# Two adds of the attention's sum over keys become one step of the instruction planner

## The chip, the cores and the metric

The kernel runs on one core of a Trainium2 chip. Its time is the device time of one execution in microseconds (us); a kernel's time is the median of several runs. The core has five engines with an instruction queue each, which start their instructions in the order of the program: TensorE (PE in the profile, with PEld for its weight loads), VectorE (DVE), ScalarE (ACT), GpSimd (POOL) and SyncE (SP), which here issues the DMAs. An engine that reaches an instruction whose input is not there yet waits, and all that stands behind it in its queue waits too.

## What is computed

The input is 2048 tokens of 640 numbers in float32. Two layers follow each other, each an attention block and a channel MLP, both with a residual. All four blocks use the same kinds of steps, and both layers the same weights:

```python
def _A_ref(x, wqkv, wo):            # attention: 32 heads of 20, window of 8 keys, every second token
    W, dil = 8, 2
    qkv = transpose((x @ wqkv).reshape(B, S, 3, H, Dh))
    q, k, v = qkv[0], qkv[1], qkv[2]
    idx = pos[:, None] - (arange(W) * dil)[None, :]       # this token and the 7 at distances 2, 4, ... 14
    kg, vg = k[idx], v[idx]                               # masked where idx < 0
    attn = softmax(where(mask, einsum("bhsd,bhswd->bhsw", q, kg) * Dh ** -0.5, -1e9))
    o = einsum("bhsw,bhswd->bhsd", attn, vg)              # the sum over the 8 keys
    return o.reshape(B, S, D) @ wo

def _B_ref(x, w1, b1, w2, b2):      # MLP 640 -> 1536 -> 640
    h = gelu(layernorm(x) @ w1 + b1)
    return h @ w2 + b2

x = x + _A_ref(layernorm(x), A_wqkv, A_wo)
x = x + _B_ref(layernorm(x), B_w1, B_b1, B_w2, B_b2)
x = x + _A_ref(layernorm(x), A_wqkv, A_wo)
x = x + _B_ref(layernorm(x), B_w1, B_b1, B_w2, B_b2)
```

## The kernel before

**Tiling.** Since the window takes every second token, even and odd tokens never meet in the attention. The tokens are cut into four units of 512, two of even and two of odd tokens (`UNITS`); on each of the 128 partitions lie four tokens of a unit that follow each other. Two layers of four units give eight steps `n` of the attention, 0 to 7, and eight of the MLP, `b`. Each `n` is split into four groups of heads (160 columns each), which makes 32 attention steps `G = 4n + g`.

**Matrix products.** TensorE works in float16. Each float32 operand is split into a high and a low half and each product is taken as three (`PASS`): high by high, high by low, low by high. Per unit TensorE does the products for q, k and v (line 648 in `qkv`), the output projection (line 805 in `project`), and the MLP in twelve blocks of 128 hidden columns: line 871 multiplies into the block, line 892 out of it. The MLPs of the last two units are done together in a scheme with seven block products instead of eight (`pair`, lines 1073 and 1108), after everything else.

**The attention on VectorE.** q, k and v go from PSUM through ScalarE (line 665) to memory and come back with DMAs that put the keys of a window beside their query (`fetch`). Function `attention(G)` then works in two halves `a` of two tokens per partition. For each half it multiplies q by the keys (line 732, 2560 columns) and sums over the 20 columns of a head (line 736); for both halves together it does the softmax with short instructions (lines 741 to 751, the exponential on ScalarE at line 747); for each half it multiplies the weights with the values (line 758, 2560 columns) and then sums over the eight keys with three adds: 8 keys to 4 (1280 columns, line 766), 4 to 2 (640 columns, line 766), 2 to 1 (320 columns, line 770, which writes the result). Each add reads what the one before wrote. There are 64 such halves, so 64 adds of each size. The result is split into high (ScalarE, line 777) and low (line 780, on GpSimd for three groups in four, on VectorE for the fourth), transposed by DMAs (`project`, line 793), and goes into the projection.

**Other work on VectorE.** Between these steps stand the low halves of the MLP's hidden block (line 882, wanted by the third pass of line 892), the low halves of the layer norm's result (line 618, which a transposing DMA at line 620 takes to TensorE), of the weights (line 476), and some residuals (lines 814 and 936).

**What sets the order.** The order on every engine is laid out before the kernel is built, by the class `Plan`. The kernel hands it steps: an engine, a planned duration, a priority, what the step needs and gives, the buffers it uses, and a function that emits its instructions. `Plan.run` keeps a clock for each engine and picks step after step. A step that needs the result of another on the same engine may start 0.06 us after the other's planned end; for any step the key by which the choice is made is not below the engine's clock plus 0.05 us:

```python
w = w + (self.LAG["sp"] + self.SPARE[o["eng"]] if moved else self.LAG[e] if e != o["eng"] else 0.06 * (e != "pe"))
...
key = (max(t - o["wait"], clock[e] + 0.05), o["prio"], o["n"])
```

So directly behind a VectorE step whose result it needs, a step comes second to any other step that is ready, whatever the priorities. A step is one item of the plan however many instructions it emits; nothing is put between them. The planned duration of a VectorE instruction of n columns is `v_cost(n)`, that is 0.067 us plus n/960 us. Steps of the kinds in `PAIRS` (all adds of the sum are among them) are kept apart in the plan from the longer GpSimd steps; a GpSimd step of this kind is placed at the end of a run of such VectorE steps and is made to wait for the VectorE step before it. After the plan, all engines run in the planned order, each waiting for the real semaphores.

Of the names in the diff, `dve(n, prio, emit, need, give, use, more)` adds a VectorE step with duration `v_cost(n) + more`; `("pv", G, a)` is the product with the values, `("ad", G, a, w)` an add, `("o", G, a)` the finished half; `vk` is the buffer `pr` with the products (two of them), `ok` the result buffer, of the `w` buffers. `FILL` and `DRAIN` are priorities of two ScalarE steps of the MLP.

Of the kernel before, what the change touches and what calls it, by code (L numbers as in the profile page):

```python
# [20 lines left out]
GC = D // NG  # L21
# [15 lines left out]
EH = 2  # L37
# [28 lines left out]
PAIRS = ("qk", "pv", "ad", "o", "sub", "at", "hlo", "yl", "xb", "ol", "wq", "lo", "lm")  # L66

TURN = 2.7
FILL, DRAIN = -420, -700

THROUGH = (("sa", 29),)
LOP = ((29, -460),)
# [209 lines left out]
def v_cost(n):  # L282
    return 0.067 + n / 960.0
# [7 lines left out]
def sliding_dilated_then_mlp_kernel(  # L291
# [18 lines left out]
    nc = tc.nc  # L310
# [41 lines left out]
    def tile_of(pool, key):  # L352
        return T[pool][plan.slot[pool, key]]
# [63 lines left out]
    def dve(n, prio, emit, need=(), give=(), use=(), more=0.0, wait=None):  # L417
        plan.add("dve", v_cost(n) + more, prio, emit, need, give, use, wait=wait, pair=give[0][0] in PAIRS)
# [26 lines left out]
    def identity():  # L445
# [7 lines left out]
        give=["b1"])  # L453
    dma(320, 41, lambda: nc.sync.dma_start(b2, bass.AP(tensor=B_b2.tensor, offset=B_b2.offset, ap=[[0, P], [1, D]])),
        give=["b2"])
# [244 lines left out]
    def attention(G):  # L700
        n, g = divmod(G, NG)
        la, u = divmod(n, NU)
        par, start, m = UNITS[u]
        E = EH * W * GC
        L = m * W * GH
        NE = m // EH
        dve = partial(any_dve, wait=HURRY.get(G))
        wk, vw, ok, hk, sk = ("qk", G), ("v", G), ("w", ("o", G)), ("ohl", n), ("sm", G)

        def ot():  # L710
            return tile_of(*ok).rearrange("p (t c) -> p t c", t=m)

        def windows(w, t0, *dims):
            c = w[:, t0:t0 + EH]
            return bass.AP(tensor=c.tensor, offset=c.offset, ap=[list(c.ap[0]), [GC, EH], *dims])

        def lg(t0=0, t1=m):
            return tile_of(*sk)[:, t0 * W * GH:t1 * W * GH].rearrange("p (t w h) -> p t w h", t=t1 - t0, w=W)

        def lgt():  # L720
            return lg().rearrange("p t w h -> p t h w")

        def mx(j):
            return tile_of(*sk)[:, L + j * m * GH:L + (j + 1) * m * GH].rearrange("p (t h) -> p t h", t=m)

        for a in range(NE):
            t0 = a * EH
            pk = ("pr", (G, a, 0))

            def qk(t0=t0, pk=pk):  # L730
                w = tile_of(*wk)
                nc.vector.tensor_mul(tile_of(*pk), w[:, HALO + m + t0:HALO + m + t0 + EH, None, :].to_broadcast([P, EH, W, GC]),  # L732
                                     windows(w, t0, [GC, W], [1, GC]))

            dve(E, G - 0.6, qk, need=[("inq", G), ("ink", G)], give=[("qk", G, a)], use=[wk, pk, sk])
            dve(E, G - 0.7, lambda pk=pk, t0=t0: nc.vector.tensor_reduce(  # L736
                lg(t0, t0 + EH).rearrange("p t w h -> p (t w h)"), tile_of(*pk).rearrange("p t w (h d) -> p (t w h) d", d=DH),
                axis=AX.X, op=OP.add), need=[("qk", G, a)], give=[("lg", G, a)], use=[pk, sk])
        last = [("lg", G, a) for a in range(NE)]
        if start == 0:  # L740
            dve(L, G - 0.8, lambda: nc.vector.tensor_add(
                lg(), lg(), mask[:, :, :, None].to_broadcast([P, m, W, GH])), need=[*last, "mask"], give=[("lm", G)], use=[sk])
            last = [("lm", G)]
        dve(L, G - 0.8, lambda: nc.vector.tensor_reduce(mx(0), lgt(), axis=AX.X, op=OP.max), need=last, give=[("mx", G)], use=[sk], more=0.19)
        dve(L, G - 0.8, lambda: nc.vector.tensor_sub(lg(), lg(), mx(0)[:, :, None, :].to_broadcast([P, m, W, GH])),
            need=[("mx", G)], give=[("sub", G)], use=[sk])
        act(L, -450 + G, lambda: nc.scalar.activation(tile_of(*sk)[:, :L], tile_of(*sk)[:, :L], AF.Exp, scale=scale),
            need=[("sub", G)], give=[("e", G)], use=[sk], table="exp")
        dve(L, G - 0.8, lambda: nc.vector.tensor_reduce(mx(1), lgt(), axis=AX.X, op=OP.add), need=[("e", G)], give=[("s", G)], use=[sk], more=0.19)
        dve(8 * m * GH // 2, G - 0.8, lambda: nc.vector.reciprocal(mx(1), mx(1)), need=[("s", G)], give=[("rc", G)], use=[sk])  # L750
        dve(L, G - 0.8, lambda: nc.vector.tensor_mul(lg(), lg(), mx(1)[:, :, None, :].to_broadcast([P, m, W, GH])),
            need=[("rc", G)], give=[("at", G)], use=[sk])
        for a in range(NE):
            t0 = a * EH
            vk = ("pr", (G, a, 1))

            def pv(t0=t0, vk=vk):
                nc.vector.tensor_mul(  # L758
                    tile_of(*vk).rearrange("p t w (h d) -> p t (w h) d", d=DH),
                    lg(t0, t0 + EH).rearrange("p t w h -> p t (w h)")[:, :, :, None].to_broadcast([P, EH, W * GH, DH]),  # L760
                    windows(tile_of(*vw), t0, [DH, W * GH], [1, DH]))

            dve(E, G - 0.85, pv, need=[("at", G), ("inv", G)], give=[("pv", G, a)], use=[vw, sk, vk])
            last = ("pv", G, a)
            for w in (4, 2):
                dve(EH * w * GC, G - 0.9, lambda vk=vk, w=w: nc.vector.tensor_add(  # L766
                    tile_of(*vk)[:, :, 0:w], tile_of(*vk)[:, :, 0:w], tile_of(*vk)[:, :, w:2 * w]),
                    need=[last], give=[("ad", G, a, w)], use=[vk])
                last = ("ad", G, a, w)
            dve(EH * GC, G - 0.9, lambda vk=vk, t0=t0: nc.vector.tensor_add(  # L770
                ot()[:, t0:t0 + EH], tile_of(*vk)[:, :, 0], tile_of(*vk)[:, :, 1]),
                need=[last], give=[("o", G, a)], use=[vk, ok])

        def hi():
            return tile_of(*hk)[:, :, 0, g * GC:(g + 1) * GC]

        act(m * GC, -350 + G, lambda: nc.scalar.activation(hi(), ot(), AF.Copy),
            need=[("o", G, a) for a in range(NE)], give=[("oh", G)], use=[ok, hk])
        def lo(eng):
            eng.tensor_sub(tile_of(*hk)[:, :, 1, g * GC:(g + 1) * GC], ot(), hi())  # L780

        if g < NG - 1:
            pool(ASIDE, -300 + G, lambda: lo(nc.gpsimd), need=[("oh", G), ("qk", G + 1, 0)], give=[("ol", G)], use=[ok, hk],
                 pair=True)
        else:
            dve(m * GC, -300 + G, lambda: lo(nc.vector), need=[("oh", G)], give=[("ol", G)], use=[ok, hk])
# [43 lines left out]
    def mlp(at, b, t0, t1):  # L830
# [5 lines left out]
        last = ("acc4", at)  # L836
# [8 lines left out]
        def rest(i):  # L845
            return M, i * REST, BANK, REST

        filled = b > 2
        put = [("put2", b, i) for i in tiles] + [("put2", b, "rest")] if filled else []

        if filled:
            for i in tiles:
                act(BANK, FILL, lambda i=i: nc.scalar.activation(accs[i], x[u][:, i, :BANK], AF.Copy, scale=WS),
                    need=[("xb", b, i)] + [("out", b - 1, NF - 1, i)] * (b > 0), give=[("put2", b, i)], use=[bank(i)])
            act(REST * M, FILL, lambda: nc.scalar.activation(
                accs[M].rearrange("p (t c) -> p t c", c=REST), x[u][:, :, BANK:], AF.Copy, scale=WS),
                need=[("xb", b, i) for i in tiles] + [("out", b - 1, NF - 1, ("rest", at - 1))], give=[("put2", b, "rest")], use=[last])

        for e in range(NF):
# [3 lines left out]
            for i, k in enumerate((ck, wk)):  # L863
                dma(328, -250 + j + 1.5 * i, lambda k=k, i=i, e=e: nc.sync.dma_start(tile_of(*k), mw[i][e]),
                    need=[("mw", e, i)], give=[k], use=[k])

            def inner(ck=ck, pk=pk):
# [8 lines left out]
               use=[yk, ck, pk])  # L876
            act(nt, -430, lambda pk=pk, h32=h32, e=e: nc.scalar.activation(  # L877
                tile_of(*h32)[:, :nt], tile_of(*pk)[:, :nt], AF.Gelu_apprx_tanh, bias=b1[:, e:e + 1], scale=1.0 / WS),
                need=[("hp", j), "b1"], give=[("h", j)], use=[pk, h32], table="gelu", ptr=1)
            act(nt, -440, lambda h32=h32, hk=hk: nc.scalar.activation(tile_of(*hk)[:, 0, :nt], tile_of(*h32)[:, :nt], AF.Copy),  # L880
                need=[("h", j)], give=[("hhi", j)], use=[h32, hk])
            dve(nt, -1000, lambda h32=h32, hk=hk: nc.vector.tensor_sub(  # L882
                tile_of(*hk)[:, 1, :nt], tile_of(*h32)[:, :nt], tile_of(*hk)[:, 0, :nt]),
                need=[("hhi", j)], give=[("hlo", j)], use=[h32, hk])
# [11 lines left out]
            if e < NF - 1:  # L896
                for i in tiles:
                    prev = [("outh", b, e - 1, i)] if e else ([("outh", b, e, i - 1)] if i > t0 else [])
                    mm(2 * D, 4, j, lambda i=i, outer=outer: outer(i, PASS[:2], [own(i), rest(i)]), need=[("hhi", j), wk, *prev] + [("put2", b, i), ("put2", b, "rest")] * (filled and e == 0),
                       give=[("outh", b, e, i)], use=[wk, hk, bank(i), last])  # L900
                    mm(D, 2, j + 0.05, lambda i=i, outer=outer: outer(i, PASS[2:], [own(i), rest(i)]),
                       need=[("hlo", j), ("outh", b, e, i)], give=[("out", b, e, i)], use=[wk, hk, bank(i), last])
# [3 lines left out]
           need=[("hhi", j), wk, *before], give=[("outh", b, e, ("rest", at))], use=[wk, hk, last])  # L906
        mm(REST * len(tiles), len(tiles), j - 0.2, lambda: [outer(i, PASS[2:], [rest(i)]) for i in tiles],
           need=[("hlo", j), ("outh", b, e, ("rest", at))], give=[("out", b, e, ("rest", at))], use=[wk, hk, last])
        for i in tiles:
            mm(2 * BANK, 2, j, lambda i=i: outer(i, PASS[:2], [own(i)]),  # L910
               need=[("hhi", j), wk, *before], give=[("outh", b, e, i)], use=[wk, hk, bank(i)])
            mm(BANK, 1, j - 0.1, lambda i=i: outer(i, PASS[2:], [own(i)]),
               need=[("hlo", j), ("outh", b, e, i)], give=[("out", b, e, i)], use=[wk, hk, bank(i)])

        if filled:
            act(REST * M, DRAIN, lambda: nc.scalar.activation(
                x[u][:, :, BANK:], accs[M].rearrange("p (t c) -> p t c", c=REST), AF.Copy, scale=1.0 / WS),
                need=[("out", b, NF - 1, ("rest", at))], give=[("xr", la + 1, u, i) for i in tiles], use=[last])
        else:
            dve(REST * (t1 - t0), -991, lambda: add(  # L920
                x[u][:, t0:t1, BANK:], accs[M][:, t0 * REST:t1 * REST].rearrange("p (t c) -> p t c", c=REST)),
                need=[("out", b, NF - 1, ("rest", at)), *[("xb", b, i) for i in tiles]], give=[("xr", la + 1, u, i) for i in tiles],
                use=[last])
        for i in tiles:
            if filled:
                act(BANK, DRAIN, lambda i=i: nc.scalar.activation(x[u][:, i, :BANK], accs[i], AF.Copy, scale=1.0 / WS),
                    need=[("out", b, NF - 1, i)], give=[("x", la + 1, u, i)], use=[bank(i)])
            else:
                dve(BANK, -990, lambda i=i: add(x[u][:, i, :BANK], accs[i]),
                    need=[("out", b, NF - 1, i), ("xb", b, i)], give=[("x", la + 1, u, i)], use=[bank(i)])  # L930
# [417 lines left out]
```

## Time and profile before

| What | us |
|---|---|
| Median of 3 runs (lowest to highest) | 1145.94 (1145.78 to 1146.62) |
| Profiled execution: its own time | 1146.3 |
| Profiled execution: span from first to last instruction | 1144.5 |
| TensorE busy | 1136.8 |
| VectorE busy | 1041.5 |
| ScalarE busy | 609.3 |
| GpSimd busy | 115.3 |

The profile is of one execution. Busy time is the time in which at least one instruction of the engine ran; instructions of one engine overlap a little, so the sum of their durations is above it. In the timeline a row gives start, duration, engine, line and operation, the buffer written and the ones read, and the shapes; rows of the same kind that follow each other are merged and carry a count (x2). The table of waits gives who waited for whom, the total in us, how often, and the longest. The chain of waits is the sequence of work that ended last, followed back from the last instruction to what released each. The granted TensorE clock is 1.00 throughout.

### The profile page before, as it was taken

To read this page: it belongs to the slowest core of one execution; us is meant where nothing else is said; L and a number is where in the kernel's file an instruction comes from. 1 tells how busy PE (TensorE), PEld (TensorE's weight loads), DVE (VectorE), ACT (ScalarE), POOL (GpSimd) and SP (SyncE) were. 2 spreads that over 40 slices of the span, in tenths; PEclk is the share of its full clock that TensorE was granted. 3 is DMA by queue.
4 is the path that set the end of the run, shared out by engine and by line. 5 is a ranking of instruction groups with operands and counts; after the bars stand their busy time and mean duration, and the time that the engine had idled before them with its cause. 6 is when DMAs were issued, how large, how long until landed. Compare 5 with 4: busy or idle time off the path is not lost.

```text
span 1144.5 us, 17537 instructions
## 1 busy us (share of the span) xinstructions
PE 1136.8 (99%) x6834; PEld 629.0 (55%) x6834; DVE 1041.5 (91%) x1028; ACT 609.3 (53%) x1133; POOL 115.3 (10%) x94
## 2 busy tenths in 40 slices
PE   9999999999999999999999999999999999999998
PEld 6444446576655465545555644556455556554476
DVE  7899999999999999999999999998999993848972
ACT  6385436636355276724627743377457445657630
POOL 1010000111101111120113011103110000000000
PEclk9999999999999999999999999999999999999999
DMA  9999999988876478567755865568677556974101
GB/s 304 300 303 265 302 341 258 307 279 247 228 236 198 131 221 220 166 202 197 189 203 175 206 191 176 179 191 183 175 207 195 194 165 156 227 246 128 42 24 69
DMA packets 239791, 235.47 MB, mean 206 GB/s; under 512 B 139020, under 2 KB 195164, under 8 KB 239708
## 3 DMA queue, kind: packets, MB, share of 16 engines
q1 hardware_dynamic: 239708, 234.36, 69.5%
q8 instruction: 53, 0.87, 0.3%
q14 instruction: 30, 0.25, 0.1%
HBM read 157.55 MB, written 44.78 MB: 177 GB/s over the span
## 4 chain that ended last, share of the span: by engine, by line
PE 91%; DVE 5%; issue 1%; ACT 1%; POOL 1%; DMA 0%; DVEq 0%; POOLq 0%; ACTq 0%
PE ps L648 34%; PE ps L871 19%; PE acc L892 19%; PE ps L805 10%; PE acc L1073 3%; PE ps L1108 3%; PE ps L1073 2%; DVE pr L1005 1%; POOL ohl L780 1%; PE acc L1269 1%; DVE pr L758 0%; DVE pr L732 0%; DVE sm L736 0%; DMA yT<-w 0%; DVE pr L766 0%
## 5 line engine op out<-in xcount | busy, mean ns | idle before, releaser
L648 PE MATMUL ps<-wq,yT 128*128 128x480 f16 (+1 forms) x1950 | 391.0, 363 | 1.3 <-ACT xf L822 0.9
L648 PEld LDWEIGHTS <-yT 128*128 128x128 f16 x1950 | 189.0, 98 | 200.4 <-issue 1.4
L892 PE MATMUL acc<-c,act 128*128 128x512 f16 (+1 forms) x1728 | 248.6, 299 | 1.3 <-DVE xf L936 1.3
L871 PE MATMUL ps<-yT,c 128*128 128x512 f16 (+1 forms) x1260 | 246.0, 349 | 0.0
L892 PEld LDWEIGHTS <-act 128*128 128x128 f16 x1728 | 135.8, 98 | 107.9 <-issue 1.6
L732 DVE TENSOR_TENSOR pr<-qk 128x2560 f32<-128x2560 f32 x64 | 181.3, 2836 | 2.1 <-DMA qk<-spill 2.1
L736 DVE TENSOR_REDUCE sm<-pr 128x128 f32<-128x2560 f32 x64 | 179.5, 2807 | 0.2
L758 DVE TENSOR_TENSOR pr<-sm,v 128x2560 f32<-128x2560 f32 x64 | 178.9, 2819 | 0.4
L871 PEld LDWEIGHTS <-c 128*128 128x128 f16 x1260 | 120.3, 98 | 106.7
L665 ACT ACTIVATE ev<-ps 128x480 f32<-128x480 f32 x128 | 72.2, 566 | 162.2 <-PE ps L648 151.0
L766 DVE TENSOR_TENSOR pr<-pr 128x640 f32<-128x640 f32 (+1 forms) x128 | 143.4, 1152 | 0.2
L805 PE MATMUL ps<-wo,yT 128*128 128x320 f16 x960 | 131.7, 299 | 0.0
L877 ACT ACTIVATE act<-ps,b 128x512 f32<-128x512 f32 (+1 forms) x84 | 52.3, 622 | 129.4 <-PE ps L871 125.0
L805 PEld LDWEIGHTS <-yT 128*128 128x128 f16 x960 | 93.7, 98 | 37.4
L780 POOL TENSOR_TENSOR ohl<-w,ohl 128x640 f16<-128x640 f32 x24 | 39.9, 1664 | 466.5 <-DVE pr L732 274.9
L882 DVE TENSOR_TENSOR act<-act 128x512 f16<-128x512 f32 (+1 forms) x84 | 51.4, 615 | 12.2 <-ACT act L880 12.1
L587 POOL TENSOR_TENSOR ln<-ln,half 128x2 f32<-128x2 f32 (+1 forms) x31 | 33.0, 1071 | 229.1 <-ACT ln L584 229.0
L625 POOL TENSOR_TENSOR xf<-xf,b 128x640 f32<-128x640 f32 x24 | 37.4, 1559 | 147.5 <-DVE ohl L780 44.9
L610 ACT ACTIVATE w<-xf,ln 128x640 f32<-128x640 f32 x53 | 47.5, 910 | 7.3 <-POOL ohl L780 4.0
L618 DVE TENSOR_TENSOR w<-w,w 128x640 f16<-128x640 f32 x56 | 44.9, 817 | 4.6 <-ACT w L616 4.4
L880 ACT ACTIVATE act<-act 128x512 f16<-128x512 f32 (+1 forms) x84 | 47.3, 565 | 3.3 <-PE acc L892 1.5
L570 ACT ACTIVATE junk<-xf 128x640 f16<-128x640 f32 x57 | 41.8, 733 | 11.4 <-DVE xf L814 8.0
(200 smaller groups left out, 990.5 us busy)
## 6 DMA issues: line engine op xcount, KB each, us to landing
c<-mw SPq DMA_DIRECT2D x174, 320.0 KB, 3.5
spill<-ev SPq DMA_DIRECT2D x64, 480.0 KB, 4.0
qk<-spill SPq DMA_DIRECT2D x32, 880.0 KB, 6.1
v<-spill SPq DMA_DIRECT2D x32, 880.0 KB, 5.2
qk<-spill SPq DMA_DIRECT2D x32, 320.0 KB, 3.6
act<-in_B_w_dram SPq DMA_DIRECT2D x24, 320.0 KB, 5.1
mw<-c SPq DMA_DIRECT2D x24, 320.0 KB, 5.7
pr<-in_B_w_dram SPq DMA_DIRECT2D x24, 320.0 KB, 4.0
```

Of the source, the lines that this page charges most:

```text
L648: nc.tensor.matmul(ps, transposed(yk)[:, a * KD + k, t * P:(t + 1) * P], wq[:, b, k, g, i0:i1], start=first and j == 0, stop=last and j == ...
L665: act(3 * GC, -400 + n, lambda i=i, pk=pk, ek=ek: nc.scalar.activation(tile_of(*ek)[:, :, i], tile_of(*pk)[:, :3 * GC].rearrange("p (a c) ...
L732: nc.vector.tensor_mul(tile_of(*pk), w[:, HALO + m + t0:HALO + m + t0 + EH, None, :].to_broadcast([P, EH, W, GC]), windows(w, t0, [GC, W], ...
L736: dve(E, G - 0.7, lambda pk=pk, t0=t0: nc.vector.tensor_reduce(lg(t0, t0 + EH).rearrange("p t w h -> p (t w h)"), tile_of(*pk).rearrange(" ...
L758: nc.vector.tensor_mul(tile_of(*vk).rearrange("p t w (h d) -> p t (w h) d", d=DH), lg(t0, t0 + EH).rearrange("p t w h -> p t (w h)")[:, :, ...
L766: dve(EH * w * GC, G - 0.9, lambda vk=vk, w=w: nc.vector.tensor_add(tile_of(*vk)[:, :, 0:w], tile_of(*vk)[:, :, 0:w], tile_of(*vk)[:, :, w ...
L805: nc.tensor.matmul(tile_of(*pk)[:, :D // 2], transposed(yk)[:, a * KD + k, t * P:(t + 1) * P], wo[:, b, k, c * D // 2:(c + 1) * D // 2], s ...
L871: nc.tensor.matmul(tile_of(*pk)[:, :nt], tile_of(*ck)[:, a, k * P:(k + 1) * P], transposed(yk)[:, c * KD + k, t0 * P:t1 * P], start=i == 0 ...
L877: act(nt, -430, lambda pk=pk, h32=h32, e=e: nc.scalar.activation(tile_of(*h32)[:, :nt], tile_of(*pk)[:, :nt], AF.Gelu_apprx_tanh, bias=b1[ ...
L882: dve(nt, -1000, lambda h32=h32, hk=hk: nc.vector.tensor_sub(tile_of(*hk)[:, 1, :nt], tile_of(*h32)[:, :nt], tile_of(*hk)[:, 0, :nt]), nee ...
L892: nc.tensor.matmul(accs[k][:, c0:c0 + n], tile_of(*hk)[:, a, (i - t0) * P:(i - t0 + 1) * P], tile_of(*wk)[:, c, w0:w0 + n], start=first, s ...
L1073: nc.tensor.matmul(tile_of(*to(i))[:, :HALF], hl()[:, a, i * P:(i + 1) * P], row(c), start=start and (a, c) == PASS[0], stop=(a, c) == PAS ...
```

## The change

The two last adds of a half, 640 and 320 columns, are handed to the planner as one step, whose function emits both instructions one behind the other. Its planned duration is the sum of the two durations, without the 0.06 us between them. The first add remains a step of its own. Instructions, shapes, buffers and what is waited for are the same as before; the three adds now stand in named functions. The number 2 in the test which MLP units have their accumulator filled from ScalarE becomes a named constant with the same value.

```diff
-FILL, DRAIN = -420, -700
+FILL, DRAIN, FILLED = -420, -700, 2
...
             dve(E, G - 0.85, pv, need=[("at", G), ("inv", G)], give=[("pv", G, a)], use=[vw, sk, vk])
             last = ("pv", G, a)
-            for w in (4, 2):
-                dve(EH * w * GC, G - 0.9, lambda vk=vk, w=w: nc.vector.tensor_add(
-                    tile_of(*vk)[:, :, 0:w], tile_of(*vk)[:, :, 0:w], tile_of(*vk)[:, :, w:2 * w]),
-                    need=[last], give=[("ad", G, a, w)], use=[vk])
-                last = ("ad", G, a, w)
-            dve(EH * GC, G - 0.9, lambda vk=vk, t0=t0: nc.vector.tensor_add(
-                ot()[:, t0:t0 + EH], tile_of(*vk)[:, :, 0], tile_of(*vk)[:, :, 1]),
-                need=[last], give=[("o", G, a)], use=[vk, ok])
+            def four(vk=vk):
+                w = tile_of(*vk)
+                nc.vector.tensor_add(w[:, :, 0:4], w[:, :, 0:4], w[:, :, 4:8])
+
+            def rest(t0=t0, vk=vk):
+                w = tile_of(*vk)
+                nc.vector.tensor_add(w[:, :, 0:2], w[:, :, 0:2], w[:, :, 2:4])
+                nc.vector.tensor_add(ot()[:, t0:t0 + EH], w[:, :, 0], w[:, :, 1])
+
+            dve(4 * EH * GC, G - 0.9, four, need=[last], give=[("ad", G, a, 4)], use=[vk])
+            dve(2 * EH * GC, G - 0.9, rest, need=[("ad", G, a, 4)], give=[("o", G, a)], use=[vk, ok], more=v_cost(EH * GC))
...
-        filled = b > 2
+        filled = b > FILLED
```

## The prediction, made before the changed kernel had run

> **What bounds the kernel now.** I read the page first, then the stretches, who waits for whom on TensorE, the chain of waits, and last the timeline around the adds. The page:
>
> ```profile
> span 1144.5 us, 17537 instructions
> PE 1136.8 (99%) x6834; PEld 629.0 (55%) x6834; DVE 1041.5 (91%) x1028; ACT 609.3 (53%) x1133; POOL 115.3 (10%) x94
> PE 91%; DVE 5%; issue 1%; ACT 1%; POOL 1%; DMA 0%; DVEq 0%; POOLq 0%; ACTq 0%
> ```
>
> TensorE is busy for all but 1144.5 − 1136.8 = 7.7 us. VectorE's 91% is an average: it has an attention part, which lasts until about 950 us, and a lighter end. The stretches (columns: length, then busy time and instructions of PE, PEld, DVE, ACT, POOL, then clock, DMA share, GB/s):
>
> ```profile
> 57.00:950.00 893.00, 890.60 (x5298) 484.80 (x5296) 871.00 (x739) 480.86 (x916) 106.79 (x76) 1.00 0.73 217
> ```
>
> There TensorE lacks 2.4 us and VectorE 22 us of 893: two queues, both nearly full, that hand work to each other. TensorE's waits (who waited for whom, total, times, longest), all of them:
>
> ```profile
> PE acc L1269 <- POOL ident L447: 1.3, 1, 1.3
> PE acc L892 <- DVE xf L936: 1.3, 1, 1.3
> PE ps L648 <- ACT xf L822: 0.9, 1, 0.9
> PE ps L1108 <- DVE wq L1182: 0.3, 1, 0.3
> PE ps L648 <- DMA yT<-w: 0.2, 1, 0.2
> ```
>
> The first is the start; the second, third and fifth (1.3 + 0.9 + 0.2 = 2.4 us) are the whole loss inside the attention part. So a change of VectorE's order can win little and lose as much as it makes TensorE wait. Where TensorE comes to depend on VectorE, the chain of waits shows it (start, us, what):
>
> ```profile
> 747.70 3.24 PE ps L871 x15
> ...
> 751.63 2.81 DVE pr L758
> ...
> 779.31 2.75 DVE pr L758
> ...
> 782.27 7.33 POOL ohl L780
> ...
> 789.62 0.02 ACT w L610
> ...
> 790.44 0.42 ACT xf L822
> ...
> 790.91 9.27 PE ps L648 x45
> ```
>
> For 40 us the end hangs on VectorE's queue, then on one GpSimd step, then on ScalarE, and TensorE starts 0.9 us late.
>
> **The change part by part.** *Instructions.* None is added or removed: 64 adds of 640 and 64 of 320 columns before and after. No step of SP or GpSimd is in the merged step, and no new semaphore wait. `FILLED` is 2 where 2 stood; it emits nothing, so there is nothing to cover.
>
> *The place of the 320 add.* In 6 of the 64 halves the 320 add now follows its own 640 add directly (the first at 158 us, the last at 400 us); in the other 58 something stands between. One with something between, and one where the two halves alternate:
>
> ```profile
> 759.10 0.81 DVE L766 TENSOR_TENSOR pr<-pr 128x640 f32<-128x640 f32 x1
> 759.84 0.68 DVE L882 TENSOR_TENSOR act<-act 128x512 f16<-128x512 f32 x1
> 760.44 0.48 DVE L770 TENSOR_TENSOR w<-pr 128x320 f32<-128x320 f32 x1
> 760.84 1.48 DVE L766 TENSOR_TENSOR pr<-pr 128x1280 f32<-128x1280 f32 x1
> ...
> 792.26 1.55 DVE L766 TENSOR_TENSOR pr<-pr 128x640 f32<-128x640 f32 x2
> 793.73 0.89 DVE L770 TENSOR_TENSOR w<-pr 128x320 f32<-128x320 f32 x2
> 794.53 0.42 DVE L741 TENSOR_TENSOR sm<-sm,mask 128x256 f32<-128x256 f32 x1
> ```
>
> The first and the last without:
>
> ```profile
> 158.16 0.82 DVE L766 TENSOR_TENSOR pr<-pr 128x640 f32<-128x640 f32 x1
> 159.02 0.49 DVE L770 TENSOR_TENSOR w<-pr 128x320 f32<-128x320 f32 x1
> ...
> 398.40 2.35 DVE L766 TENSOR_TENSOR pr<-pr 128x1280 f32<-128x1280 f32 x2
> 400.79 0.49 DVE L770 TENSOR_TENSOR w<-pr 128x320 f32<-128x320 f32 x1
> ```
>
> Before an unrelated instruction the 640 add takes 759.84 − 759.10 = 0.74 us of the queue, though it lasts 0.81: the next one starts into its tail. Before its own 320 add it takes 159.02 − 158.16 = 0.86 us. The dependent one waits for the end, which costs 0.12 us. After the change all 64 pairs are of this sort: 58 × 0.12 = 7.0 us more on VectorE's queue. The plan does not see them, since its duration for the step is the bare sum.
>
> The Trainium skill, page "VectorE: DVE Perf Modes", section "The DRAIN you can't avoid", says that after every VectorE operation the next one does not start until the pipeline is empty, with or without a semaphore. By that rule it is the same what follows the 640 add, the 7.0 us would be zero and the sum would lose its first two terms below. The trace disagrees (0.74 against 0.86 us), and the measurement decides.
>
> *What of the 7.0 us reaches the end.* VectorE's own waits between 57 and 950 us swallow a delay where they are for something paced by TensorE:
>
> ```profile
> DVE act L882 <- ACT act L880: 5.4, 8, 1.4
> DVE pr L732 <- DMA qk<-spill: 2.1, 2, 1.6
> ```
>
> That is 7.5 us of cover, spread over ten places, as much as the 7.0; the delay is cut back at each and does not pile up. Two places lie outside this cover. From 634 us until the wait at 791 us VectorE waits for nothing: there 10 pairs add 10 × 0.12 = 1.2 us. The stretch ends in the chain shown, whose last link already makes TensorE late, so I take all of it. The other is where TensorE meets the transposed layer norm without any slack:
>
> ```profile
> 368.10 4.84 DMA yT<-w
> ...
> 372.99 24.48 PE ps L648 x120
> ```
>
> The transposes wait for line 618 on VectorE; the two pairs just before (346 and 349 us) add 0.24, part of which the wait of line 882 at 356 us takes back: 0.2 us. If the cover is gone in the new order, the term is the full 7.0.
>
> *The projections.* Where the halves alternated, both results were done 2 × 0.74 + 2 × 0.40 = 2.28 us after the first 640 add started; now it is 2 × (0.86 + 0.40) = 2.52 us: 0.24 us later for the split, for the four transposes on SP and for the loads queued behind them there. The tightest projection, in SP's and PE's timeline and the DMA table (median us to landing last):
>
> ```profile
> 767.66 6.46 SPq L793 DMA_TRANSPOSE yT<-ohl  x4
> 773.53 16.46 PE L805 MATMUL ps<-wo,yT 128*128 128x320 f16 x120
> yT<-ohl SPq DMA_TRANSPOSE x32, 3.8
> ```
>
> The first lands about 767.7 + 3.8 = 771.5, 2 us before use. With 0.24 of the pair and about 1.2 of the stretch it still fits: nothing. Without this slack it would be up to 1.4.
>
> *What stood between.* In 15 of the 58 places it is line 882. Behind the merged step it comes up to 0.40 + 0.12 = 0.5 us later. TensorE does a whole block of line 871 (3.24 us above) between two blocks of line 892, and shows no wait for line 882, so I put it at nothing; without that cover it is 0.5 us each time, 7.5 at most.
>
> *A new order.* A merged step cannot be split by one that is ready, so from the first such place on every later choice of the plan can come out differently, on all queues. What stalls the plan did not foresee comes anew. The trace has one sample, 2.4 us in 893. A GpSimd step of the paired kind shows how large one can be:
>
> ```profile
> L780 POOL TENSOR_TENSOR ohl<-w,ohl x24: 1396/1402/7315, 72.9 to 930.2; 128x640 f16<-128x640 f32 x24
> ```
>
> It takes 1.4 us, and once, beside two products of line 758 in a row (the chain above), 7.3; of the 5.9 us excess 0.9 reached TensorE. Bounds for the new order: all three waits gone, −2.4; or all of TensorE's 4.0 us once more and the 7.0 uncovered on top. For the likeliest I take one late VectorE step of the sort of line 936 more (1.3) and half a jam (0.4): 1.7, an estimate, nearer to the waits that are there than to the far bound, because they are what this kind of plan has left.
>
> *Sum.* 1.2 + 0.2 + 1.7 = 3.1 us. The profiled execution took 1146.3, 1.8 more than its span and 0.4 more than the median 1145.94; that becomes 1149.4, and the median 1149.0.
>
> **The rivals.** *No change that can be measured.* About 0.2% (2.3 us) is what a measurement of this kernel tells from no change. If the new order's stalls are no larger than the old ones, there remain 1.2 + 0.2 = 1.4 us: 1147.3. For it: 7.5 us of cover, 2 us of slack at the projection. Against: the stretch from 634 to 791 us without cover. A variant of its own is that the dependent add costs nothing, because the 0.12 us is an effect of the rows picked; then only the order counts, and with stalls as large as before the time is 1145.9. The six rows with 0.85 or 0.86 us against all others speak against it. The rule of the page named above would make it so.
>
> *Faster.* One mechanism: the jam at 782 us. It needs the GpSimd step beside two products in a row; the merged steps move the ends of VectorE's runs, at which the plan places GpSimd steps, and finish the first half's result earlier (0.86 + 0.40 = 1.26 us after its 640 add starts instead of 0.74 × 2 + 0.40 = 1.88), which lets the first result buffer go 0.6 us sooner. If the jam is gone and the waits at lines 892 and 648 with it, 2.4 us go: 1143.5. It decides only if nearly all three go. Against it: the 0.12 us per pair remain, and the tail cannot give, since VectorE there only follows TensorE:
>
> ```profile
> 1141.16 0.49 DVE L936 SCALAR_TENSOR_TENSOR xf<-acc,xf 128x320 f32<-128x320 f32 x1 [1.95 <-PE acc L1073]
> ```
>
> *Much slower.* The new order puts a projection or a load on TensorE's path before VectorE can feed it, and all 7.0 us count, with a second set of TensorE's waits: 1145.94 + 7.0 + 4.0 = 1156.9. For it: both queues are nearly full. Against: ten places of cover.
>
> **How the numbers follow.** The forecast (some 3 us slower) has 0.40, much slower 0.14, no measurable change 0.26 (0.05 of it for an add that costs nothing) and faster 0.20. Thus faster 0.20, same 0.26, slower 0.54. The range reaches from the faster bound with the wait at line 1108 gone too (1145.94 − 2.4 − 0.3 = 1143.2) to 1157. The likeliest case alone reaches from 1148.3, where it can be told from no change, to 1153 (the sum with all of 4.0 instead of 1.7, and 1.4 for the projection).
>
> **What would show it.** Right: each 320 add starts 0.86 us behind its own 640 add, 64 times; 1028 VectorE instructions as before; a longer list of TensorE's waits, in sum near 7 instead of 4.0 us; TensorE's busy time unchanged near 1137. The step on the cover is wrong if VectorE's waits for line 880 stay at 5.4 us while TensorE's grow. The step on the bubble is wrong if the spacing stays 0.74. The prediction is wrong if TensorE's waits fall below 4 us (then the order, not the bubble, decided and was better), or if a single new stall exceeds 5 us.

## The result and the profile after

The changed kernel took 1149.66 us (median of 15 executions, 1147.05 to 1153.40) against 1146.38 us for the kernel before on the same chip (15 executions, 1145.37 to 1148.24). The ratio is 1.0034, 95% interval 1.0026 to 1.0041: 0.34% slower. With the experiments it was measured again: 1153.22 us (7 executions, 1147.97 to 1154.33), ratio 1.0045, interval 1.0029 to 1.0060. By the medians the two measurements are 3.3 and 6.8 us over the kernel before. The executions of the changed kernel spread over 6 us, above 1150 us lie 7 of the 15 and 4 of the 7, and so the median depends on how many of these a measurement happens to hold.

The profile was taken of an execution of 1147.59 us. Its page, and the stretch from 57 to 950 us (columns as before: length, busy time and count of PE, PEld, DVE, ACT, POOL, then clock, DMA share, GB/s):

```profile
span 1145.8 us, 17535 instructions
PE 1136.6 (99%) x6834; PEld 629.1 (55%) x6834; DVE 1046.0 (91%) x1028; ACT 612.8 (53%) x1135; POOL 115.4 (10%) x94
```
```profile
57.00:950.00 893.00, 889.17 (x5289) 484.51 (x5288) 874.94 (x739) 484.16 (x918) 106.94 (x76) 1.00 0.74 217
```

As many instructions on VectorE, the same work on TensorE (1136.6 us); VectorE is busy 4.5 us longer, and TensorE lacks 3.8 us in this stretch instead of 2.4. The pairs, in the timeline of VectorE and in the groups of its line 772:

```profile
629.03 0.82 DVE L771 TENSOR_TENSOR pr<-pr 128x640 f32<-128x640 f32 x1
629.88 0.49 DVE L772 TENSOR_TENSOR w<-pr 128x320 f32<-128x320 f32 x1
630.29 0.82 DVE L618 TENSOR_TENSOR w<-w,w 128x640 f16<-128x640 f32 x1
```
```profile
L772 DVE TENSOR_TENSOR w<-pr 128x320 f32<-128x320 f32 x64 | 31.5, 492 | 2.5
```

The 320 add starts 0.85 us behind its 640 add. VectorE's idle time in front of them is 2.5 us in all (last column), where the kernel before had 0.2; the rest of the 0.12 us is the overlap that is lost. TensorE's waits in this execution, then in a second profile of the same kernel, of an execution of 1153.26 us:

```profile
PE acc L895 <- ACT act L883: 1.9, 1, 1.9
PE acc L1272 <- POOL ident L447: 1.4, 1, 1.4
PE acc L895 <- ACT acc L858: 0.8, 1, 0.8
PE ps L808 <- ACT ps L820: 0.7, 1, 0.7
PE ps L874 <- DMA c<-mw: 0.4, 1, 0.4
PE ps L1111 <- DVE wq L1185: 0.3, 1, 0.3
```
```profile
PE ps L808 <- ACT ps L820: 3.2, 1, 3.2
PE acc L895 <- ACT act L883: 1.9, 1, 1.9
PE acc L895 <- DVE xf L939: 1.7, 1, 1.7
PE acc L1272 <- POOL ident L447: 1.4, 1, 1.4
PE ps L648 <- DMA yT<-w: 1.3, 2, 0.9
PE acc L895 <- ACT acc L858: 0.6, 1, 0.6
PE ps L1111 <- DVE wq L1185: 0.4, 1, 0.4
```

The sums are 5.5 and 10.5 us, against 4.0 before. Two of the waits of before (residuals at line 936, and the one that ended the jam at 791 us) are gone in the first execution; in their place stand others that end on ScalarE. When line 808 starts, the second execution is 5.6 us behind the first (646.57 against 640.93 us). Of these 2.6 are there already at 622 us, with waits of 1.7 and 0.9 us at 270 and 376 us that the first does not have; the rest comes between. The chain of the wait of line 808 in the second starts at a GpSimd step of the layer norm:

```profile
626.56 6.41 POOL ln L587
632.97 0.02 issue
633.00 0.35 ACT ln L592 x2
...
646.19 0.34 ACT ps L820
646.53 0.04 issue
646.57 8.45 PE ps L808 x61
```

The step has two columns and a median of 0.70 us in this kernel. Here it took 6.40 us; in the first execution 2.26. In both it starts while VectorE is in the second of two products of line 758. In the first it ends at 626.27, just after VectorE has gone on to its next instruction at 626.23. In the second it ends only when VectorE's queue has run dry, behind the 320 add at 632.44, for a wait of 3 us:

```profile
622.71 5.56 DVE L758 TENSOR_TENSOR pr<-sm,v 128x2560 f32<-128x2560 f32 x2
628.18 0.69 DVE L885 TENSOR_TENSOR act<-act 128x512 f16<-128x512 f32 x1
628.78 2.89 DVE L767 TENSOR_TENSOR pr<-pr 128x1280 f32<-128x1280 f32 x2
631.58 0.82 DVE L771 TENSOR_TENSOR pr<-pr 128x640 f32<-128x640 f32 x1
632.44 0.49 DVE L772 TENSOR_TENSOR w<-pr 128x320 f32<-128x320 f32 x1
635.92 0.82 DVE L618 TENSOR_TENSOR w<-w,w 128x640 f16<-128x640 f32 x1 [2.99 <-ACT w L616]
```

ScalarE waits for it, the fills of line 820 stand behind in ScalarE's queue, and TensorE waits for them. The Trainium skill, page "VectorE: DVE Perf Modes", section "Two Vector instructions with no wait between them", says that the second tensor input of a VectorE instruction is read through an interface shared with GpSimd. The rows agree in so far as all instructions from 622.71 to 632.44 us read two tensors each, and the GpSimd step ended only behind the last of them. Why it got in between two of them in the first execution, after 2.26 us, and not in the second, they do not show: in both it started 3.85 us behind the first of the two products.

### The profile page after: what moved, and what is told of

It reads as the page before. It is cut to its first block, busy times and chain, and to the rows that moved or that the text cites. A ratio compares the mean times of both kernels' runs of the same rounds, so it can differ in the third digit from the quotient of the medians.

```text
span 1145.8 us, 17535 instructions
## 1 busy us (share of the span) xinstructions
PE 1136.6 (99%) x6834; PEld 629.1 (55%) x6834; DVE 1046.0 (91%) x1028; ACT 612.8 (53%) x1135; POOL 115.4 (10%) x94
## 4 chain that ended last, share of the span: by engine, by line
PE 90%; DVE 4%; ACT 3%; DMA 2%; issue 1%; POOL 0%; SPq 0%; POOLq 0%; DVEq 0%; ACTq 0%
PE ps L648 34%; PE acc L895 18%; PE ps L874 18%; PE ps L808 11%; PE acc L1076 3%; PE ps L1111 3%; PE ps L1076 2%; DMA c<-mw 1%; DVE pr L1008 1%; DMA yT<-w 1%; PE acc L1272 1%; DVE pr L758 0%; PE acc L1111 0%; ACT L747 0%; DVE yT L1023 0%
## 5 line engine op out<-in xcount | busy, mean ns | idle before, releaser
L758 DVE TENSOR_TENSOR pr<-sm,v 128x2560 f32<-128x2560 f32 x64 | 181.5, 2859 | 0.4
L767 DVE TENSOR_TENSOR pr<-pr 128x1280 f32<-128x1280 f32 x64 | 94.8, 1504 | 0.1
L783 POOL TENSOR_TENSOR ohl<-w,ohl 128x640 f16<-128x640 f32 x24 | 42.3, 1763 | 418.4 <-DVE pr L732 207.8
L625 POOL TENSOR_TENSOR xf<-xf,b 128x640 f32<-128x640 f32 x24 | 41.6, 1737 | 173.2 <-DVE act L885 61.7
L771 DVE TENSOR_TENSOR pr<-pr 128x640 f32<-128x640 f32 x64 | 52.5, 820 | 0.2
L587 POOL TENSOR_TENSOR ln<-ln,half 128x2 f32<-128x2 f32 (+1 forms) x31 | 26.7, 867 | 252.7 <-ACT ln L584 228.7
```

Source lines behind the costliest of these rows:

```text
L758: nc.vector.tensor_mul(tile_of(*vk).rearrange("p t w (h d) -> p t (w h) d", d=DH), lg(t0, t0 + EH).rearrange("p t w h -> p t (w h)")[:, :, ...
L767: nc.vector.tensor_add(w[:, :, 0:4], w[:, :, 0:4], w[:, :, 4:8])
L771: nc.vector.tensor_add(w[:, :, 0:2], w[:, :, 0:2], w[:, :, 2:4])
```

## The experiments

The theory at first: the 0.12 us per pair make VectorE late, and TensorE waits for it. The rival: the new order of all queues makes the loss, and the adjacency is swallowed.

**Adjacency alone.** The plan and with it the order of TensorE, ScalarE and SP are those of the kernel before; only VectorE's 640 adds are moved.

```diff
-    for o in plan.run():
+    order = list(plan.run())
+    for G in range(N * NG):
+        for a in range(M // EH):
+            step = next(o for o in order if o["give"][0] == ("ad", G, a, 2))
+            order.remove(step)
+            order.insert(next(i for i, o in enumerate(order) if o["give"][0] == ("o", G, a)), step)
+    for o in order:
```

> The kernel before, its order on TensorE, ScalarE and SP untouched; only the 640 add of each half is moved on VectorE to directly ahead of its own 320 add. Theory (the 0.12 us per pair makes VectorE late): 1.4 to 3 us over the kernel before, and TensorE's waits longer by about as much. Rival (the new order of all queues makes the loss): within 0.5 us of the kernel before, the delay swallowed by VectorE's own waits.

> The kernel before with every 640 add directly ahead of its 320 add, once more, for the profile of another execution and more times: 1150 to 1155. If the executions differ by the GpSimd step near 626 us, the profile of a slow one shows that step over 5 us; if by the lower clock after a long wait of TensorE, a wait of 3 us or more and a granted clock under 1.

Measured: 1153.40 us (5 executions, 1150.66 to 1154.59), ratio 1.0059, interval 1.0046 to 1.0072; and again 1152.73 us (7 executions, 1148.12 to 1153.92), ratio 1.0043, interval 1.0027 to 1.0060. So in the old order the adjacency by itself costs 5 to 7 us. It is not swallowed: VectorE's waits for line 880 were 5.4 us in the kernel before, and in the two profiles here they are

```profile
DVE act L882 <- ACT act L880: 5.9, 8, 1.4
```
```profile
DVE act L882 <- ACT act L880: 3.9, 6, 1.0
```

The first profile's chain of waits shows at one place how a late add comes back to VectorE as a wait:

```profile
351.14 0.50 DVE w L770
351.64 0.02 issue
351.67 0.74 ACT ohl L777
...
354.15 1.28 ACT L877
...
356.85 0.53 ACT act L880
357.38 0.02 issue
357.40 0.69 DVE act L882
```

Line 880 stands on ScalarE behind line 777, which waits for the 320 add (with two loads of tables, 1.28 us each, on the way, the second of them in the rows). What VectorE then waits for is late because VectorE was. The chain of the second profile (1152.73 us) shows the other half:

```profile
786.72 7.32 POOL ohl L780
...
794.89 0.43 ACT xf L822
795.31 0.04 issue
795.36 4.68 PE ps L648 x14
```

The same GpSimd step took 7.3 us in the kernel before too, but TensorE waited only 0.9 us then; now it waits 3.5. In the first profile (1150.66 us) the step took 3.77 us and there is no wait at this place. The part of the expectation on the step near 626 us was wrong (2.2 us there in the second profile); it was this other step, and the clock, below.

**Half of the adjacency.** The same edit with `for a in range(1)`: 32 halves.

> The kernel before with its order, the 640 add moved directly ahead of its 320 add in the first half of each attention step alone: 32 halves instead of 64, about 3.5 us of VectorE's time instead of 7. Theory A (each 0.12 us comes through): about 3.5 us over the kernel before. Theory B (a threshold, since VectorE's own waits swallow a part): below 1.5 us over it. If the GpSimd step jams here too: 5 us or more.

Measured: 1151.78 us (1150.45 to 1154.39), ratio 1.0047, interval 1.0035 to 1.0059. Half of the 0.12 us costs as much as all of them, within the intervals. So the loss does not go by the sum: its profile has one wait of 3.5 us at 795 us, behind the same GpSimd step (7.31 us).

The rows ahead of this place show why 32 halves are enough here. In the kernel before, the two products of line 758 beside which this GpSimd step gets stuck start 5.71 us behind the first product of line 805 on TensorE (779.24 against 773.53 us). With half of the adjacency it is 8.27 us, with all of it 8.25 in both profiles. For ScalarE now waits for VectorE a little earlier, where it did not in the kernel before, and the step of line 817 for which TensorE waits 0.3 us at line 805 stands behind in ScalarE's queue:

```profile
768.89 0.42 ACT L747 ACTIVATE sm<-sm 128x256 f32<-128x256 f32 x1 [1.64 <-DVE sm L745]
```

So there are some 2.5 us of slack between the two engines at this place. Once VectorE is later than that, TensorE is late with it; the stuck step, whose end is 2.5 us later against TensorE, then costs 3.5 instead of 0.9 us, with half of the pairs as with all.

**The new order alone, first try.** The changed kernel; its merged step is emitted as two, and the 320 add put behind the next VectorE instruction, whichever that is.

```diff
     for o in plan.run():
+        # the merged step becomes its two parts, one behind the other
...
+    for last in [o for o in order if o["give"][0][0] == "o"]:
+        i = order.index(last)
+        j = next((j for j in range(i + 1, len(order)) if order[j]["eng"] == "dve"), None)
+        between = order[i + 1:j + 1]
...
+        order.insert(j, order.pop(i))
```

> The changed kernel with its new order on all other engines, but in 47 of the 64 halves the 320 add is put behind the next VectorE instruction, so that 47 x 0.12 = 5.6 us of VectorE's time come back. Theory (lateness of VectorE): most of the 3.3 us comes back, 0 to 1 us over the kernel before. Rival (new order): still 2.5 to 3.5 us over it.

Measured: 1159.66 us (1153.93 to 1161.29), ratio 1.0106, interval 1.0089 to 1.0123: slower than everything else. It says nothing on the question, since in 16 halves the instruction put between reads 2560 columns, and the result comes 2.6 us later for ScalarE's queue. What this lateness alone costs is not shown either, since the GpSimd step of line 587 took 6.39 us in this profile, and TensorE waited 4.0 us behind it.

**The new order alone, second try.** Only instructions planned at up to 0.9 us are let in between, or the 640 add goes one place earlier.

```diff
-        if any(mine & held(o) or last["give"][0] in o["need"] or o.get("behind") is last for o in between):
+        if order[j]["dur"] > 0.9 or any(mine & held(o) or last["give"][0] in o["need"] or o.get("behind") is last for o in between):
+            k = order.index(prev)
+            h = next(h for h in range(k - 1, -1, -1) if order[h]["eng"] == "dve")
+            if not any(prev["need"][0] in o["give"] for o in order[h:k]):
+                order.insert(h, order.pop(k))
             continue
```

> The changed kernel's order on all other engines; on VectorE one instruction that fits is put between the 640 and the 320 add of 60 of the 64 halves (nothing longer than 0.9 us, or the 640 add one place earlier), so that 4 pairs are adjacent instead of 64 and some 7 us of VectorE's time come back. Theory (adjacency makes VectorE late and that is the loss): within 1 us of the kernel before, 1145.5 to 1147.5. Rival (the new order by itself costs): 2.5 us or more over it.

Measured: 1148.10 us (12 executions, 1146.94 to 1153.99), ratio 1.0025, interval 1.0011 to 1.0038. By the medians 1.8 us of the loss stay without the adjacency, by the ratio 2.9 (1.3 to 4.4): the new order has its own price. Three of the twelve executions still lie above 1152. VectorE's own order is not that of the changed kernel here, since an instruction stands between the two adds.

One part of the price can be seen. Every profile with this order, with and without adjacency, has a wait of TensorE at 227 to 230 us, of 1.9 us in five of them and 4.4 in the first try, and the kernel before has none there. In the changed kernel:

```profile
222.47 0.57 ACT ev L665
...
226.08 0.84 ACT act L880 x2
226.92 0.31 ACT act L883
227.23 0.05 issue
227.28 1.26 PE acc L895 x8
```

From TensorE's products of line 648 on, this chain runs through ScalarE's queue alone (two loads of tables, 1.28 us each, are in between), and no add of VectorE is in it. Between these products and those of line 892 (895 in the changed kernel) the kernel before has 45 products of line 871 on TensorE; the new order has 30.

**The GpSimd step.** The changed kernel; the 1280 add behind the two products near 625 us is made to wait for the GpSimd step, so that VectorE cannot go on until it is done.

```diff
+        if o["give"][0] == ("rr", ("a", 6), 0):
+            late = o
+        if late and o["eng"] == "dve" and o["give"][0] == ("ad", 19, 0, 4):
+            tc.add_manual_dep(o["ins"], late["ins"].name, ..., reason="port")
+            late = 0
```

> The changed kernel with one wait added: the 1280 add that follows the GpSimd step of line 587 near 625 us waits for that step, so that VectorE is idle for it at most about 1 us. Theory (the spread of the executions is that GpSimd step, 2.3 us in one execution and 6.4 in another, stuck behind VectorE): the step takes under 2 us, executions within 3 us of each other, median 1147 to 1149. Rival (the spread comes from elsewhere): median and spread of 6 us as in the changed kernel.

Measured: 1148.97 us (11 executions, 1148.05 to 1149.60), ratio 1.0021, interval 1.0013 to 1.0030. The spread falls from 6 us to 1.6. The step took 2.25 us in its profile, a little over the expected 2, and VectorE was held for less than 0.1 us.

None of the 11 executions lies above 1150 us, where 7 of 15 and 4 of 7 of the changed kernel do. So in the changed kernel it takes this step being stuck to get there; one such execution was profiled. The wait of 1.7 us at 270 us is in this profile too, in an execution of 1148.70 us.

**Both.** The second try with this wait added.

> The changed kernel's order, 60 of the 64 pairs apart again, and the added wait that lets the GpSimd step near 625 us in: what is left is the new order alone. Beside the changed kernel with the added wait alone (1148.97 us), the difference is what the 0.12 us per pair cost in this order without the stuck step. If the adjacency counts: 1 to 2 us below it, 1147 to 1148. If the new order is all: the same 1149 within 0.5 us.

Measured: 1148.94 us (7 executions, 1147.42 to 1151.82), ratio 1.0031, interval 1.0020 to 1.0042. Against the kernel with the wait alone (1.0021) nothing is gained: in the new order, with the step let in, the adjacency itself costs nothing that can be measured. Where its time goes, VectorE's waits between 57 and 950 us show: they are 16.8 us in sum here and 11.5 in the kernel with the wait alone, those for line 883 (892 here) 4.1 and 2.3:

```profile
DVE act L894 <- ACT act L892: 4.1, 8, 1.2
```
```profile
DVE act L885 <- ACT act L883: 2.3, 7, 0.5
```

So of the 60 × 0.12 = 7.2 us some 5.3 are taken by waits that get shorter. A spread of 4 us is left here, whose place the one profile, of the shortest execution, does not show.

**A plan that knows the 0.12 us.**

```diff
-...give=[("o", G, a)], use=[vk, ok], more=v_cost(EH * GC))
+...give=[("o", G, a)], use=[vk, ok], more=v_cost(EH * GC) + 0.12)
```

> The changed kernel with 0.12 us added to the planned duration of the merged step, so that the plan sees the adjacency; all 64 pairs remain adjacent. Theory (the loss is that the plan's order relies on a VectorE that is earlier than the real one): at most 1.5 us over the kernel before. Rival (VectorE's time itself is lost, planned or not): 3 to 7 us over it.

Measured: 1148.69 us (11 executions, 1147.57 to 1150.50), ratio 1.0019, interval 1.0010 to 1.0027. That is 2.4 us over the kernel before, more than the 1.5 of the theory and less than the rival's 3. All pairs are adjacent and the plan counts it, and the loss is about that of the new orders without adjacency.

**Other orders.** Two changes of the plan's arithmetic alone, 0.0671 for 0.067 in `v_cost`, and 0.07 for 0.06 us between dependent steps of one engine.

> The kernel before with 0.0671 for 0.067 us in the plan's duration of a VectorE instruction: no instruction is changed, only the plan's arithmetic in its fourth digit. Theory (lateness): within 0.5 us of the kernel before, since no pair becomes adjacent by it. Rival (any new order costs): 1 to 5 us over it.

> The kernel before with 0.07 for 0.06 us between a VectorE step and one that needs its result, in the plan alone. The order comes out different on all engines (784 lines of TensorE's order against 836 for the change), and 6 pairs are adjacent as before. If any new order costs: 1 to 4 us over the kernel before. If only the adjacency costs: within 0.7 us of it.

The first did not do what its label says: the order came out the same on every engine, so it is a repeat of the kernel before, at 1146.68 us (11 executions), ratio 1.0001, interval 0.9993 to 1.0010. The second is a new order, with 6 adjacent pairs: 1147.51 us (11 executions, 1146.95 to 1149.94), ratio 1.0015, interval 1.0007 to 1.0024. Its largest waits of TensorE are others than those of either kernel: 1.9 us for line 855 (858 in the changed kernel, where it is 0.8) and 1.4 for line 882.

**The kernel before, with its GpSimd step let in.** The same kind of wait, at the products at 780 us.

```diff
+        if o["give"][0] == ("ol", 24):
+            port = o
+        if port and o["eng"] == "dve":
+            tc.add_manual_dep(o["ins"], port["ins"].name, ..., reason="port")
+            port = None
```

> The kernel before with one wait added: the VectorE step behind the two products at 780 us waits for the GpSimd step of line 780 that took 7.3 us there. If that step's being stuck is what makes TensorE wait 0.9 us at 791 us: the step takes under 3 us, the wait goes, 0.3 to 0.9 us below the kernel before. If VectorE's added idle time costs as much as it saves: within 0.3 us.

Measured: 1145.37 us (11 executions, 1144.32 to 1146.71) against 1146.09, ratio 0.9995, interval 0.9986 to 1.0003. The longest of these steps is 3.77 us instead of 7.32, somewhat over the expected 3, and TensorE's wait for line 822 is gone from its list. The median is 0.7 us lower, which the interval does not tell from nothing.

## Why the prediction was right, and where its steps were not

The forecast of 1149.0 us, 0.27% over 1145.94, came out: 1149.66, which is 3.3 us over the kernel before measured beside it, where 3.1 were forecast. That it came so near is in part luck. The same kernel measured again gave 1153.22, since the median hangs on how many executions have the stuck step, and the terms of the sum fared differently.

*The bubble on VectorE,* 0.12 us for each of 58 more pairs: right. The spacing is 0.85 us in the median of all 64 (0.85 to 0.93), where 55 of the 58 pairs before had the next instruction after 0.73 or 0.74. The section that the prediction sets against this is not contradicted by the trace: the Trainium skill, page "VectorE: DVE Perf Modes", section "The DRAIN you can't avoid", adds in the same paragraph that a next operation that is not held starts earlier.

*The cover that takes most of it.* In the changed kernel's order this held: with the GpSimd step let in, VectorE's waits shrink by 5.3 of the 7.2 us and the time is the same (1148.97 against 1148.94). In the old order, from whose profile the cover was read, it did not: with the adjacency alone the waits for line 880 are still 3.9 to 5.9 us while 5 to 7 us are lost, since they go round through ScalarE's queue, where line 880 stands behind steps that wait for VectorE.

*The 1.2 + 0.2 us that come through.* In the changed kernel this term cannot be told from nothing. Between the new order alone (1.0025) and the changed kernel (1.0034 and 1.0045) lie 1.0 to 2.3 us, not clear of the intervals, and nothing is left of them with the GpSimd step let in. The stretch from 634 to 791 us, on which the 1.2 rested, ends in no wait of TensorE in either profile after. (VectorE does wait once in that stretch before, 0.56 us at 634 us.) Of the meeting at 372 us, on which the 0.2 rested, one profile after shows a wait of 0.9 us at 376 and the other none.

*The new order, 1.7 us.* The size was about right: 1.8 us by the medians (2.9 by the ratio) for the changed kernel's order without adjacency, 1.4 for an order that differs for another reason. The stall was of another kind than the late VectorE step like that of line 936 from which the size was taken: a wait of 1.9 us behind ScalarE's queue alone. That a new draw costs was argued from what waits there are; the orders without adjacency and the plan that knows the 0.12 us came out 0.15 to 0.31% slower.

*Half a jam, 0.4 us.* The mechanism was seen, its size was off. GpSimd's stuck step makes TensorE wait 0.7 or 3.2 us in the changed kernel, by the execution, and moves the median by 0.7 us (1149.66 against 1148.97 with the step let in) to 4.2 us (1153.22).

*What was to be seen.* TensorE's waits in sum near 7: 5.5 in one execution and 10.5 in another. TensorE's busy time near 1137: 1136.6. Of the waits of VectorE for line 880, 5.4 us before, 2.0 are left (line 883 there), so the sign that the cover is wrong did not show.

The rival "no change" is excluded by the interval, "faster" as well; "much slower", with the 7.0 us on the path, comes near to what the adjacency does in the old order (5 to 7 us). The two causes do not add: adjacency alone in the old order costs at least as much as both together (1.0059 and 1.0043 against 1.0034 and 1.0045).

What stays open: what decides in an execution whether a GpSimd step gets in between two VectorE instructions or is stuck; where the 4 us of spread arise that are left in the new order without adjacency; and whether half of the pairs cost as much as all elsewhere than at the one place shown.

## What to carry to other kernels

A dependent instruction put directly behind its source costs the tail of the source, 0.12 us here, and a planner that is not told of it lays out the other engines for a VectorE that is earlier than the real one. Whether that costs time is a matter of the order around it: 5 to 7 us in one order here, nothing measurable in another. Before counting an engine's waits as cover for a delay, follow what they wait for back: if that stands, in another engine's queue, behind a result of the first engine, the wait moves with the delay. And where two engines are nearly full, any new order is a new draw: measure some orders that differ for no reason before giving a loss of 0.2% to the edit.

## What the runs showed of the hardware that was not expected

A GpSimd step of two columns, 0.7 us long, took 6.4 us beside VectorE instructions with two tensor inputs, and in another execution of the same program 2.3 us at the same place.

A long wait of TensorE can cost more than itself, and not each time. Two kernels with a wait of 3.48 us, both at 795 us (the half and the full adjacency; stretch, length, TensorE's busy time and count, granted clock, DMA share, GB/s):

```profile
795.00:800.00 5.00, 4.89 (x25) 1.00 0.36 69
```
```profile
795.00:800.00 5.00, 4.64 (x15) 0.66 0.39 75
```

In the second the granted clock was 0.66 for 5 us, about 0.34 × 5 = 1.7 us lost. After the wait of 3.2 us in the changed kernel it stayed at 1.00. In the first try of the new order alone, waits of 4.4 and 4.0 us were each followed by 5 us at 0.66 (from 230 and from 650 us). The Trainium skill, page "TensorE: Matmul & The Clock Gate", section "Part 1: The HAM clock gate (the "warmup" mystery)", says that the clock drops after an idle window of some 3.4 us, and that the windows run freely. The rows agree: no drop behind the 3.2 us, one behind one of the two waits of 3.48 us, one behind each of the longer ones. In executions of the changed kernel that were not profiled there may be drops too: their mean granted clock is 0.998 in 4 of the 15 and in 3 of the 7.
